# The opening of the full-attention layers: the first operands loaded ahead, the shift row written to SBUF, and the last keys and values cut into smaller pieces

## The chip, the cores and the metric

The kernel runs on one core of a Trainium2 chip. The metric is the device time of one execution in microseconds (us). The engines named below are PE (TensorE: matmuls), PEld (its weight loads), ACT (ScalarE), DVE (VectorE), POOL (GpSimd) and SP (SyncE), which here issues the DMAs.

## The reference

Four layers are chained: a windowed attention layer (A), a full one (B), then A and B again with the same weights. S = 2048 positions, D = 512, H = 32 heads of 16.

```python
def _B_ref(x, wqkv, wo):
    B, S, D = x.shape
    H = 32; Dh = D // H
    qkv = (lambda x, *d: x.transpose(*d))((x @ wqkv).reshape(B, S, 3, H, Dh), 2, 0, 3, 1, 4)
    q, k, v = qkv[0], qkv[1], qkv[2]
    scores = jnp.einsum("bhqd,bhkd->bhqk", q, k) * scale
    p = _softmax(scores, axis=-1)
    o = jnp.einsum("bhqk,bhkd->bhqd", p, v)
    return (lambda x, *d: x.transpose(*d))(o, 0, 2, 1, 3).reshape(B, S, D) @ wo
...
x = x + _A_ref(_layernorm(x, axis=-1), A_wqkv, A_wo)
x = x + _B_ref(_layernorm(x, axis=-1), B_wqkv, B_wo)
x = x + _A_ref(_layernorm(x, axis=-1), A_wqkv, A_wo)
x = x + _B_ref(_layernorm(x, axis=-1), B_wqkv, B_wo)
```

`_A_ref` is the same with a mask: a query sees itself and the 255 positions before it.

## The kernel before

**Tiling.** The positions are cut into 4 chunks of 512 (`c`), the heads into 4 head tiles of 8 (`ht`, `t`) or 8 quads of 4 (`qd`); two quads make a head tile. A projection of one chunk for one head tile is a pass of 12 matmuls (`mms`, L390: 4 slices of D times 3 products of split half-precision numbers). Q and K of a chunk are four such passes (`project`, L478); values (`values`, L607) go by four tiles of 128 positions, 12 matmuls each over all 32 heads (512 columns) or over a half of them (256 columns; `halves`, where 0 is the lower heads, used by quads 0 to 3, and 1 the upper).

**Keys, queries and the shift row.** Q and K are written to DRAM (`qs`, `kf`) in a layout of 64 rows a head (`R`), and loaded back by quad. Row 7 of a head in `kf` holds a shift, a bound from the largest squared norm of a key, that keeps the exponential in range. So the scores of a head cannot start before all keys of that head are known: `keys` (L553) leaves behind a piece of work in the list `pend`, which squares and sums the head's rows on PE (`squares`, L535) and reduces them on DVE to `KM` (L562); `settle` (L591) runs such pieces; `key_shift` (L595) takes the maximum over the chunks, makes the row `mk` (L602) and writes it to `kf` (L604). `queries` does the same for the query's own bound, a row `m` in `qs` (L588). `m` and `mk` share one buffer (tag "m").

**Full attention.** For a quad `load_full` (L744) loads `qt` (L748) and `kt` in two halves of 1024 keys (L752; three buffers). `attn_full` goes in 16 steps of 128 keys: two score groups on PE (L727), two exponentials on ACT (L735, 128x1024 each), and the products with V (L779). One layer has 4 x 8 x 16 = 512 steps and 1024 exponentials. Layer 1 goes by chunk of queries, then by quad; layer 3 by head tile, chunk, quad.

**Side work.** Work that isn't attention (projections, output projections, norms, for this layer or the next) is a list of `Work` generators. `Side` puts pieces of it between the attention steps: in a full layer `share` hands out a budget a step (`least`, 0.33 us of matmul by the code's own cost MM = 0.222 a pair), each pass writing into the one bank `halves`, which DVE reads out (`join`, L415 and L416). `finish` runs what is left without attention beside it, and `all_of` does that for a whole list. Weights of a work are loaded when it opens; there are two weight buffers, so a work opens when the one two before it is done. PE's order is the order in which this Python code issues; in the full layers DVE's too. The other engines, SP among them, are ordered by the planner.

**The way from a windowed layer to a full one.** After the last windowed attention the works of `tails[l]` and then `lasts[l]` run with no attention beside them: what depends on the output projection of chunk 3, its norm ("N") and its transposes ("T", DMA transposes at L470), and what else was put there. Then `key_shift` writes the row for all heads (layer 1) or for head tile 0 (layer 3, whose other tiles get theirs during the attention through `shift3`). Then the full attention begins with a load of `qt` and `kt`.

```python
tails = {0: [VV(1, 2, True, (0,)), OO(0, 3, True), VV(1, 1, True, (0,), late(1)), Q(1, 1, True, late(1)), T(1, 3), K(1, 3)],
         2: [VV(3, 0, True, (0,)), OO(2, 3, True), VV(3, 1, True, (0,), late(3)), VV(3, 2, True, (0,), late(3)), Q3(0, 0, True, late(3)), T(3, 3), K3(3, 0, True)]}
lasts = {0: [VV(1, 3)], 2: [VV(3, 3, True, (0,)), VV(3, 0, True, (1,))]}
```

`VV(l, c, act, halves, after, tiles)` are values, `OO(l, c)` the output projection of chunk c with the norm for the next layer, `Q` and `K` all four passes of a chunk, `Q3` and `K3` one pass (one head tile) with a slice of the weights.

Of the kernel before, what the change touches and what calls it, by code (L numbers as in the profile page):

```python
# [19 lines left out]
P = 128  # L20
# [4 lines left out]
QC = 512  # L25
# [164 lines left out]
def fast_path(ctx, tc, flag, a_x, a_wqkv, a_wo, b_wqkv, b_wo, out):  # L190
# [287 lines left out]
    def project(l, s, c, act, ht=None):  # L478
# [3 lines left out]
        w = weights(ty, s, n, *((0, D, 0) if ht is None else (ht * P, (ht + 1) * P, not act)))  # L482
# [112 lines left out]
    def key_shift(l, ht=None):  # L595

        settle()
        r = quarters(ht)
        kx = vp.tile([P, 1], F32, name=f"kx{l}_{ht}", tag="kx")
        nc.vector.tensor_reduce(kx[r], KM[l][r], axis=AX.X, op=ALU.max)  # L600
        m = vp.tile([P, QC], F16, name=f"mk{l}_{ht}", tag="m", bufs=1)
        nc.vector.tensor_scalar(m[r], ones[r], kx[r], -0.515, op0=ALU.mult, op1=ALU.mult)  # L602
        for t in range(NHT) if ht is None else (ht,):
            nc.sync.dma_start(rows(kf)[8 * t:8 * t + 8, 7, :].rearrange("h (c n) -> h c n", n=QC),  # L604
                              m[32 * t:32 * t + 8, None, :].broadcast_to([8, NQ, QC]))

    def values(l, c, act, halves=(0, 1), tiles=range(4)):  # L607
# [136 lines left out]
    def load_full(l, c, qd):  # L744
        n = f"{l}_{c}_{qd}"
        pair = slice(2 * qd, 2 * qd + 2)
        qt = pp.tile([P, 2, QC], F16, name=f"qt{n}", tag="qt", bufs=2)
        nc.sync.dma_start(qt, qs[1, c][pair].rearrange("r p n -> p r n"))  # L748
        kts = []
        for v in range(2):  # L750
# [69 lines left out]
    class Work:  # L820
# [34 lines left out]
        proj = property(lambda self: self.name is not None and self.name[0] in ("K", "Q", "K3", "Q3"))  # L855
# [130 lines left out]
    def attention(l, works):  # L986
# [5 lines left out]
        for t in range(NHT if l == 3 else 1):  # L992
            for c in range(NQ):
                qds = range(2 * t, 2 * t + 2) if l == 3 else range(NQD)
                if l == 1:

                    sd = sd or Side(NT * NQD // 2, works[0], works[1], 0.33)
                    while ("Q", 1, c) not in DONE:
                        sd.one(True)
# [4 lines left out]
                for qd in qds:  # L1004
                    if (l, c, qd) == (1, 0, NQD // 2):
                        sd.finish()
                        sd = Side(NT * NQD * NQ - NT * NQD // 2, works[1], works[2], 0.33)
                    nxt = load(l, c, qd + 1) if qd + 1 in qds else None
                    a = acc[qd % 2 if win else 0]
                    began, u = clock[0], 0  # L1010
                    for f in (attn_win if win else attn_full)(l, c, qd, *ops, a):
# [15 lines left out]
                        elif u:  # L1027
                            sd.step()
                        drain()
# [5 lines left out]
                if not win:  # L1035
                    settle()
# [14 lines left out]
    def K3(c, ht, act=False):  # L1051
        return Work(later(keys, 3, c, act, ht), PK / 4, ("K3", c, ht), [("T", 3, c)], True, ring=not act)
# [3 lines left out]

    def shift3(ht):
        def gen():
            key_shift(3, ht)
# [104 lines left out]

    def side1():
        m = [(ty, s) for ty in range(2) for s in range(4)]
        a = [CW(*x, [("C", *y)] if y else [("Q", 1, 2)]) for y, x in zip([None] + m, m)]
        a += [Q(1, c, False) for c in (2, 3)]
# [4 lines left out]
    def side3(t, c):  # L1173
        a = [Q3(c + 1, t)] if c < 3 else []
# [6 lines left out]
        if (t, c) != (0, 0):  # L1181
# [3 lines left out]
    works = [[side0(c) for c in range(NQ)], [[upper(1, c) for c in range(3)], side1()], [side2(c) for c in range(NQ)],  # L1185
             [side3(t, c) for t in range(NHT) for c in range(NQ)]]
    late = lambda l: [("N", l, 3)]
    tails = {0: [VV(1, 2, True, (0,)), OO(0, 3, True), VV(1, 1, True, (0,), late(1)), Q(1, 1, True, late(1)), T(1, 3), K(1, 3)],
             2: [VV(3, 0, True, (0,)), OO(2, 3, True), VV(3, 1, True, (0,), late(3)), VV(3, 2, True, (0,), late(3)), Q3(0, 0, True, late(3)), T(3, 3), K3(3, 0, True)]}
    lasts = {0: [VV(1, 3)], 2: [VV(3, 3, True, (0,)), VV(3, 0, True, (1,))]}  # L1190
    for l in range(4):
        if l % 2 == 0:
            attention(l, works[l] + [tails[l]])
            all_of(tails[l], lasts[l])
            key_shift(l + 1, 0 if l else None)
            all_of(lasts[l], works[l + 1][0])
        else:
# [43 lines left out]
```

## Time and profile before

| | us |
|---|---|
| three timed runs | 2759.93, 2760.06, 2761.41 (median 2760.06) |
| the profiled execution | 2759.5 |
| its span, first to last instruction | 2757.7 |
| PE busy | 2496.1 |
| ACT busy | 2362.9 |
| of it the exponentials (L735, 2432 of them) | 2238.8 |

The span starts at 0 in the profile's views. Rows of the timeline are: start, duration (both us), engine, line, operation, output and inputs, shapes, count of merged instructions, and in brackets the idle time ahead of it with what ended it. "SPq" rows are the issue of DMAs, not the transfers. Matmuls are pipelined: a matmul's duration is longer than the distance to the next.

### The profile page before, as it was taken

What the parts mean: (1) busy time and instruction counts of PE and PEld (TensorE: products, weight loads), DVE (VectorE), ACT (ScalarE), POOL (GpSimd) and SP (SyncE); (2) the same over time, 40 slices, a digit from 0 to 9 for tenths busy, and PEclk for the clock granted to TensorE, in tenths of its full rate; (3) what the DMA queues carried; (4) which work ended last, traced back from release to release, by engine and by line L of the source; (5) the groups of instructions that cost most, each with busy time, mean ns of one, the idle gap of its engine ahead of it and who ended that gap; (6) DMA issues with size and microseconds to landing.
All of it is one profiled execution on the core that took longest, in us unless ns stands there. A gap on an engine that the chain in (4) does not pass through costs nothing.

```text
span 2757.7 us, 112292 instructions
## 1 busy us (share of the span) xinstructions
PE 2496.1 (91%) x50513; PEld 1100.3 (40%) x50513; DVE 1094.9 (40%) x2314; ACT 2362.9 (86%) x2683; POOL 515.8 (19%) x1074
## 2 busy tenths in 40 slices
PE   7888989999989999999998898899899999998987
PEld 3233334444433344444443333534444444433332
DVE  5564554122343335325326566323333333333333
ACT  4556654899999999999995667399999999999997
POOL 1445552001000000100105678100000000000000
PEclk9999999999999999999999999999999999999999
DMA  8888856322342224324225565623232333333332
GB/s 286 226 241 240 244 178 191 96 83 82 100 120 79 86 93 137 102 78 126 93 73 169 157 181 143 175 72 109 84 107 90 98 97 104 112 104 123 114 120 103
DMA packets 335035, 359.67 MB, mean 130 GB/s; under 512 B 113616, under 2 KB 250320, under 8 KB 328144
## 3 DMA queue, kind: packets, MB, share of 16 engines
q1 hardware_dynamic: 334544, 352.40, 42.3%
q8 instruction: 397, 6.50, 1.0%
q14 instruction: 94, 0.77, 0.1%
HBM read 239.60 MB, written 96.99 MB: 122 GB/s over the span
## 4 chain that ended last, share of the span: by engine, by line
ACT 56%; PE 23%; issue 11%; DVE 5%; DMA 3%; POOL 2%; SPq 0%; ACTq 0%; DVEq 0%; POOLq 0%
ACT e L735 55%; PE b L402 10%; PE acc L812 3%; PE acc L779 3%; PE bs L402 2%; PE s L731 2%; PE s L727 2%; PE b L399 1%; POOL e L802 1%; POOL e L805 1%; DMA qt<-qs 1%; DMA kt<-kw 0%; DMA wr<-in_A_wo_dram 0%; DVE ot L694 0%; DMA w<-wd 0%
## 5 line engine op out<-in xcount | busy, mean ns | idle before, releaser
L735 ACT ACTIVATE e<-s 128x1024 f32<-128x1024 f32 (+2 forms) x2432 | 2238.8, 1058 | 121.0 <-PE s L731 95.3
L779 PE MATMUL acc<-e,vt 64*17 64x512 f32 x16384 | 1085.0, 590 | 1.3 <-issue 1.3
L727 PE MATMUL s<-qt,kt 64*32 64x512 f16 x16384 | 849.0, 380 | 130.4 <-ACT e L735 106.6
L727 PEld LDWEIGHTS <-kt 64*32 64x32 f16 x16384 | 406.7, 89 | 944.2 <-issue 868.8
L779 PEld LDWEIGHTS acc<-e,vt 64*17 64x17 f32 x16384 | 280.5, 92 | 61.1 <-issue 1.5
L805 POOL TENSOR_SCALAR_AFFINE_SELECT e<-e 128x256 f32<-128x256 f32 x512 | 224.9, 446 | 196.5 <-ACT e L735 195.4
L802 POOL TENSOR_SCALAR_AFFINE_SELECT e<-e 128x256 f32<-128x256 f32 x448 | 198.1, 449 | 114.1 <-ACT e L735 112.3
L712 POOL TENSOR_TENSOR oh<-o,oh 128x512 f16<-128x512 f32 x31 | 36.1, 1165 | 938.1 <-DVE oh L711 884.8
L812 PE MATMUL acc<-e,vt 128*17 128x384 f32 (+2 forms) x2816 | 204.7, 396 | 5.3 <-POOL e L802 4.0
L731 PE MATMUL s<-qt,kt 64*128 64x384 f16 (+2 forms) x1408 | 129.0, 280 | 64.0 <-ACT e L735 38.2
L415 DVE TENSOR_SCALAR sa<-acc 128x512 f32<-128x512 f32 x64 | 44.3, 692 | 335.4 <-PE acc L779 335.4
L402 PE MATMUL b<-xc,w 128*128 128x512 f16 x696 | 166.1, 390 | 7.0 <-DMA w<-wd 5.8
L677 DVE SCALAR_TENSOR_TENSOR x<-b,x 128x512 f32<-128x512 f32 x122 | 83.9, 688 | 193.0 <-PE b L399 189.8
L402 PEld LDWEIGHTS <-w 128*128 128x128 f16 x816 | 77.4, 100 | 122.8 <-issue 35.8
L521 POOL TENSOR_TENSOR sq<-sp 128x512 bf16<-128x512 f16 x28 | 41.0, 1463 | 442.2 <-DVE sp L515 427.6
L506 ACT ACTIVATE sp<-b 128x512 f16<-128x512 f32 x58 | 34.7, 598 | 103.3 <-PE b L402 91.2
L731 PEld LDWEIGHTS <-kt 64*128 64x128 f16 x1408 | 54.4, 94 | 167.6 <-issue 137.0
L521 POOL TENSOR_TENSOR sq_h<-sp_h 128x512 bf16<-128x512 f16 x27 | 40.1, 1484 | 409.8 <-DVE sp_h L515 409.8
L399 PE MATMUL b<-wo,oh 64*32 64x512 f16 x2592 | 109.9, 376 | 6.2 <-DVE x L677 3.1
L399 PE MATMUL b<-xc,w 64*32 64x512 f16 x2688 | 110.9, 376 | 3.0 <-DVE j L416 2.3
L399 PE MATMUL b<-xc,w_h 64*32 64x512 f16 x2592 | 104.4, 376 | 4.1 <-DVE km L562 3.9
L415 DVE TENSOR_SCALAR j_h<-b 128x512 f32<-128x512 f32 x27 | 18.7, 691 | 218.7 <-PE b L399 187.6
(136 smaller groups left out, 1874.8 us busy)
## 6 DMA issues: line engine op xcount, KB each, us to landing
kt<-kf SPq DMA_DIRECT2D x128, 512.0 KB
qt<-qs SPq DMA_DIRECT2D x128, 256.0 KB
xd<-x SPq DMA_DIRECT2D x96, 256.0 KB
x<-xd SPq DMA_DIRECT2D x96, 256.0 KB
w<-wd SPq DMA_DIRECT2D x22, 1024.0 KB
kt<-kw SPq DMA_DIRECT2D x64, 256.0 KB
qs<-sp SPq DMA_DIRECT2D x48, 256.0 KB
wo<-wd SPq DMA_DIRECT2D x12, 1024.0 KB
```

Of the source, the lines that this page charges most:

```text
L399: nc.tensor.matmul(ps[g:g + 32, r], a[k, g:g + 32], b[k], start=(i == 0), stop=(i == len(pairs) - 1), skip_group_check=True)
L402: nc.tensor.matmul(ps, a, b, start=(i == 0), stop=(i == len(pairs) - 1))
L415: nc.vector.tensor_scalar(dst, ps[0], scale, None, op0=ALU.mult)
L521: nc.gpsimd.tensor_tensor(sq, sp[:, 0], sp[:, 0], ALU.mult)
L677: nc.vector.scalar_tensor_tensor(xs[i], p, 1 / WS, xs[i], op0=ALU.mult, op1=ALU.add)
L727: nc.tensor.matmul(ps[g:g + 32, h], kt[R * h:R * h + R, pr, kc + g:kc + g + 32], qt[R * h:R * h + R, pr], start=True, stop=True, skip_grou ...
L731: nc.tensor.matmul(ps[:, h, s0:s0 + wd_], kt[R * h:R * h + R, pr, kc:kc + P], qt[R * h:R * h + R, pr, qc:qc + wd_], start=True, stop=True)
L735: nc.scalar.activation(e[:, :, w0:w1], ps[:, :, w0:w1], AF.Exp, scale=SCALE)
L779: nc.tensor.matmul(acc[r][32 * h:32 * h + DH + 1, :], V[l, qd // 4, j // 8][k, j % 8, 4 * (qd % 4) + h, :], es_[h // 2][k, h % 2, :], star ...
L802: nc.gpsimd.affine_select(v, v, pattern=[[0, 2], [-1, P]], compare_op=ALU.is_gt, fill=0.0, base=0, channel_multiplier=1)
L805: nc.gpsimd.affine_select(v, v, pattern=[[0, 2], [1, P]], compare_op=ALU.is_ge, fill=0.0, base=0, channel_multiplier=-1)
L812: nc.tensor.matmul(a[32 * h:32 * h + DH + 1, q * P:(q + nb) * P], V[l, (4 * c + j) // 4][:, j % 4, 4 * qd + h, :], es_[h // 2][:, h % 2, s ...
```

## The change

Four things, for both full layers:

1. `keys` gets an argument `then`, which is called with the head tile once its squares are reduced. A new work `K1(ht)` does the keys of layer 1's chunk 3 for one head tile and calls `key_shift` for it; `K3` does so for chunk 3 of head tile 0. `key_shift` works on one head tile at a time.
2. `early_keys` loads the first 1024 keys of the first quad into `kt` before the tail works, without a valid row 7. `early_queries` loads the first `qt`. For head tile 0 `key_shift` writes the row into that tile in SBUF (two DMAs, partitions 7 and 71) and then to `kf` as before; its row `mk` has a buffer of another tag. `load_full` takes what has been loaded.
3. The order of the tails. Layer 1: the values of chunk 1 with both halves and the upper values of chunk 0 come before the transposes of chunk 3; K of head tiles 0 and 1 follow, and two tiles of the lower values of chunk 3. Q of chunk 1, K of head tiles 2 and 3, two lower value tiles and the upper values of chunk 3 go to the attention's side work. Layer 3: the order of five works, and two lower value tiles of chunk 3 go to the side work.
4. Loops in `attention` run side work until what a quad needs is there: the shift of head tile 1, 2 or 3 before the load of quad 2, 4 or 6 of layer 1's first chunk, and the last two value tiles before step 11 of the first quad. `settle` isn't called while a pass is under way (`PH["busy"]`), and `values` calls it between tiles outside of attention.

```diff
-    def keys(l, c, act, ht=None):
+    def keys(l, c, act, ht=None, then=None):
...
                 nc.vector.tensor_reduce(KM[l][r, c:c + 1], ph[r], axis=AX.XY if PH["full"] else AX.X, op=ALU.max)
+                if then is not None:
+                    then(l, ht)
...
-    def key_shift(l, ht=None):
-
-        settle()
+    def key_shift(l, ht):
+
         r = quarters(ht)
         kx = vp.tile([P, 1], F32, name=f"kx{l}_{ht}", tag="kx")
         nc.vector.tensor_reduce(kx[r], KM[l][r], axis=AX.X, op=ALU.max)
-        m = vp.tile([P, QC], F16, name=f"mk{l}_{ht}", tag="m", bufs=1)
+        if PH["full"]:
+            m = vp.tile([P, QC], F16, name=f"mk{l}_{ht}", tag="m", bufs=1)
+        else:
+            m = vp.tile([P, QC], F32, name=f"mk{l}_{ht}", tag="j").bitcast(F16)[:, :QC]
         nc.vector.tensor_scalar(m[r], ones[r], kx[r], -0.515, op0=ALU.mult, op1=ALU.mult)
-        for t in range(NHT) if ht is None else (ht,):
-            nc.sync.dma_start(rows(kf)[8 * t:8 * t + 8, 7, :].rearrange("h (c n) -> h c n", n=QC),
-                              m[32 * t:32 * t + 8, None, :].broadcast_to([8, NQ, QC]))
+        if ht == 0:
+            early_queries(l)
+            for pr in range(2):
+                nc.sync.dma_start(PRE["k"][7:P:R, pr, :].rearrange("r (c n) -> r c n", n=QC),
+                                  m[2 * pr:2 * pr + 2, None, :].broadcast_to([2, 2, QC]))
+        nc.sync.dma_start(rows(kf)[8 * ht:8 * ht + 8, 7, :].rearrange("h (c n) -> h c n", n=QC),
+                          m[32 * ht:32 * ht + 8, None, :].broadcast_to([8, NQ, QC]))
+        DONE["S", l, ht] = clock[0]
+
+    PRE = {}
+
+    def early_keys(l):
+
+        PRE["k"] = pp.tile([P, 2, S // 2], F16, name=f"kt{l}_0_0_0", tag="kt", bufs=3)
+        nc.sync.dma_start(PRE["k"], kf[0:2, :, :S // 2].rearrange("r p n -> p r n"))
+
+    def early_queries(l):
+
+        if "q" not in PRE:
+            PRE["q"] = pp.tile([P, 2, QC], F16, name=f"qt{l}_0_0", tag="qt", bufs=2)
+            nc.sync.dma_start(PRE["q"], qs[1, 0][0:2].rearrange("r p n -> p r n"))
...
+            if not PH["full"] and not PH["win"]:
+                settle(False)
             yield -us if PH["full"] else -12 * us
...
-                    while ("Q", 1, c) not in DONE:
+                    while ("Q", 1, c) not in DONE or pend and PH["busy"]:
                         sd.one(True)
...
+                    while (l, c, qd % 2) == (1, 0, 1) and qd + 1 in qds and ("S", 1, (qd + 1) // 2) not in DONE:
+                        if ("K1", (qd + 1) // 2) in DONE and not PH["busy"]:
+                            settle()
+                        else:
+                            sd.one(True)
                     nxt = load(l, c, qd + 1) if qd + 1 in qds else None
...
+                        while not win and (c, qd, u) == (0, 0, NT - 5) and ("V", l, 3, (0,), 2) not in DONE:
+                            sd.one(True)
...
-                if not win:
+                if not win and not PH["busy"]:
                     settle()
...
+    def K1(ht, act=False):
+        return Work(later(keys, 1, NQ - 1, act, ht, key_shift), PK / 4, ("K1", ht), [("T", 1, NQ - 1), ("P", 1, 1)], True)
...
+    def last_lower(l):
+
+        return VV(l, 3, False, (0,), (), range(2, 4))
...
-        a += [Q(1, c, False) for c in (2, 3)]
+        a += [Q(1, c, False) for c in (1, 2, 3)]
...
     def side3(t, c):
-        a = [Q3(c + 1, t)] if c < 3 else []
+        a = [last_lower(3)] if (t, c) == (0, 0) else []
+        a += [Q3(c + 1, t)] if c < 3 else []
...
-    works = [[side0(c) for c in range(NQ)], [[upper(1, c) for c in range(3)], side1()], [side2(c) for c in range(NQ)],
+    works = [[side0(c) for c in range(NQ)], [[last_lower(1), K1(2), upper(1, 2), upper(1, 3), K1(3)], side1()], [side2(c) for c in range(NQ)],
...
-    tails = {0: [VV(1, 2, True, (0,)), OO(0, 3, True), VV(1, 1, True, (0,), late(1)), Q(1, 1, True, late(1)), T(1, 3), K(1, 3)],
-             2: [VV(3, 0, True, (0,)), OO(2, 3, True), VV(3, 1, True, (0,), late(3)), VV(3, 2, True, (0,), late(3)), Q3(0, 0, True, late(3)), T(3, 3), K3(3, 0, True)]}
-    lasts = {0: [VV(1, 3)], 2: [VV(3, 3, True, (0,)), VV(3, 0, True, (1,))]}
+    tails = {0: [VV(1, 2, True, (0,)), OO(0, 3, True), VV(1, 1, True, (0, 1), late(1)), VV(1, 0, True, (1,), late(1)), T(1, 3), K1(0, True), K1(1, True)],
+             2: [VV(3, 0, True, (0,)), OO(2, 3, True), Q3(0, 0, True, late(3)), VV(3, 1, True, (0,), late(3)), VV(3, 2, True, (0,), late(3)), VV(3, 0, True, (1,), late(3)), T(3, 3), K3(3, 0, True)]}
+    lasts = {l: [VV(l + 1, 3, True, (0,), (), range(2))] for l in (0, 2)}
...
             attention(l, works[l] + [tails[l]])
+            settle()
+            early_keys(l + 1)
+            if l == 0:
+                early_queries(1)
             all_of(tails[l], lasts[l])
-            key_shift(l + 1, 0 if l else None)
             all_of(lasts[l], works[l + 1][0])
+            settle()
```

More of the change, by code (lines that the diff above doesn't have):

```diff
@@ L481, in project @@
         ty, n = l % 2, f"{l}_{s}_{c}" + ("" if ht is None else f"_h{ht}")
-        w = weights(ty, s, n, *((0, D, 0) if ht is None else (ht * P, (ht + 1) * P, not act)))
+        w = weights(ty, s, n, *((0, D, 0) if ht is None else (ht * P, (ht + 1) * P, l == 3 and not act)))
         yield wait(8)
@@ L854, in fast_path @@
         done = begun = open = going = False
[L855 removed]
+        proj = property(lambda self: self.name is not None and self.name[0] in ("K", "Q", "K1", "K3", "Q3"))
         adds = property(lambda self: self.w and (self.name is None or self.name[0] == "N"))
@@ L1051, in K3 @@
     def K3(c, ht, act=False):
-        return Work(later(keys, 3, c, act, ht), PK / 4, ("K3", c, ht), [("T", 3, c)], True, ring=not act)
+        return Work(later(keys, 3, c, act, ht, key_shift if c == NQ - 1 and ht == 0 else None), PK / 4, ("K3", c, ht), [("T", 3, c)], True, ring=not act)
     def Q3(c, ht, act=False, after=()):
         return Work(later(queries, 3, c, act, ht), PK / 4, ("Q3", c, ht), [("T", 3, c), *after], True, ring=not act)
+    def K1(ht, act=False):
+        return Work(later(keys, 1, NQ - 1, act, ht, key_shift), PK / 4, ("K1", ht), [("T", 1, NQ - 1), ("P", 1, 1)], True)
     def shift3(ht):
         def gen():
+            settle()
             key_shift(3, ht)
```

12 lines of the change are left out of this document (7 added, 5 removed).

## The prediction

> **What bounds the kernel now.** First the page: its busy shares and the chain of waits.
>
> ```profile
> span 2757.7 us, 112292 instructions
> PE 2496.1 (91%) x50513; PEld 1100.3 (40%) x50513; DVE 1094.9 (40%) x2314; ACT 2362.9 (86%) x2683; POOL 515.8 (19%) x1074
> ACT e L735 55%; PE b L402 10%; PE acc L812 3%; PE acc L779 3%; PE bs L402 2%; PE s L731 2%; PE s L727 2%; PE b L399 1%; POOL e L802 1%; POOL e L805 1%; DMA qt<-qs 1%; DMA kt<-kw 0%; DMA wr<-in_A_wo_dram 0%; DVE ot L694 0%; DMA w<-wd 0%
> ```
>
> Over half of the chain is the exponential (L735). Next, the waits of ACT and of PE inside layer 1's attention (496 to 1448 us):
>
> ```profile
> ACT e L735 <- PE s L727: 7.1, 11, 1.7
> PE s L727 <- ACT e L735: 43.7, 119, 1.1
> PE b L399 <- DVE j L416: 3.0, 4, 0.8
> ```
>
> (Who waited for whom: us in total, times, longest.) In 952 us ACT waits for scores 11 times, 7.1 us in all: a full layer lasts as long as its 1024 exponentials. So the change can act at two places, where no exponential runs: from the last one of a windowed layer to the first of the full layer behind it. I read both in the timeline. Between layers 0 and 1:
>
> ```profile
> 432.00 4.82 ACT L735 ACTIVATE e<-s 128x1024 f32<-128x1024 f32 x5
> 439.04 1.48 PE L402 MATMUL bs<-wv,xc 128*128 128x256 f16 x12
> 454.65 1.47 PE L402 MATMUL bs<-wv,xc 128*128 128x256 f16 x12
> 460.12 2.76 PE L402 MATMUL bs<-xc,w 128*128 128x512 f16 x12
> 462.71 2.75 PE L402 MATMUL b<-xc,w 128*128 128x512 f16 x12
> 471.79 2.75 PE L402 MATMUL bs<-xc,w 128*128 128x512 f16 x12 [1.14 <-DMA xc<-xh]
> 484.09 0.38 PE L546 MATMUL b<-sq,hsum 128*32 128x512 bf16 x1 [1.02 <-ACT sq L519]
> 484.40 2.76 PE L402 MATMUL bs<-wv,xc 128*128 128x512 f16 x12
> 485.88 1.41 SPq L604 DMA_DIRECT2D kf<-mk_None  x4
> 489.60 1.41 SPq L752 DMA_DIRECT2D kt<-kf  x3
> 494.86 0.62 PE L727 MATMUL s<-qt,kt 64*32 64x512 f16 x16
> 495.51 24.86 ACT L735 ACTIVATE e<-s 128x1024 f32<-128x1024 f32 x27
> ```
>
> The last exponential ends at 436.82 and the next starts at 495.51: 58.7 us, in which PE is almost never idle (1.14 and 1.02 us). It is a queue of projections: values of chunk 2, output projection, values of chunk 1 (from 454.65), Q of chunk 1 (460.12), K of chunk 3 (471.79), values of chunk 3 (484.40). A pass of 12 matmuls over 512 columns takes 462.71 - 460.12 = 2.59 us; one over 256 columns half of it, 1.3 us. Between layers 2 and 3 the picture is another:
>
> ```profile
> 1725.09 1.94 ACT L735 ACTIVATE e<-s 128x1024 f32<-128x1024 f32 x2 [0.47 <-PE s L731]
> 1732.25 1.48 PE L402 MATMUL bs<-wv,xc 128*128 128x256 f16 x12
> 1748.05 0.53 SPq L370 DMA_DIRECT2D wv<-wd  x1
> 1757.25 0.69 DVE L448 TENSOR_TENSOR xh<-xn,xh 128x512 f16<-128x512 f32 x1
> 1765.56 4.45 PE L402 MATMUL bs<-xc,w_h 128*128 128x512 f16 x12 [3.79 <-DMA x<-xd]
> 1771.35 0.38 PE L546 MATMUL bs<-sq_h,hsum 128*32 128x512 bf16 x1 [1.03 <-ACT sq_h L519]
> 1774.48 0.34 DVE L602 TENSOR_SCALAR mk<-ones,kx 32x512 f16<-32x512 f16 x1 [1.86 <-DMA qs<-m]
> 1777.53 1.41 SPq L752 DMA_DIRECT2D kt<-kf  x3
> 1783.07 0.63 PE L727 MATMUL s<-qt,kt 64*32 64x512 f16 x16 [0.75 <-DMA kt<-kf]
> 1783.61 4.69 ACT L735 ACTIVATE e<-s 128x1024 f32<-128x1024 f32 x5 [0.87 <-PE s L727]
> ```
>
> Here 56.6 us pass from 1727.03 to 1783.61. K of the last chunk starts 3.79 us late and in 4.45 us instead of 2.59, the shift row waits 1.86 us for its tile, and the first scores wait for the load of `kt` behind the shift row. That load and two weight loads, in the chain of waits:
>
> ```profile
> 454.84 5.22 DMA w<-wd
> 1755.22 3.42 DMA w_h<-wd
> 1777.53 5.49 DMA kt<-kf
> ```
>
> 1 MB of weights takes 5.22 us and a 256 KB slice 3.42; a half-width `wv` (512 KB) I put between, at 4.
>
> **Layer 1's start, step by step.** Values of chunk 2 and the output projection stay: PE is at 454.65. Values of chunk 1 with both halves are 4 x 2.59 = 10.4, upper values of chunk 0 4 x 1.3 = 5.2: 470.3. In this time the norm and the transposes of chunk 3, which landed at 471.7 before, are done; two 1 MB weight loads no longer run beside them, so I take them as hidden under the 5.2 (if not, +1.4). K of head tiles 0 and 1, 2.59 each. The ring has two buffers: tile 0's slice is asked for at 465.1 (in time); tile 1's at 470.3, so at 473.7 + 0.1, 0.9 after tile 0 ends at 472.9; it ends at 476.4. Tile 0's squares stand behind it on PE (0.4). From squares to shift row the old rows show 485.88 - 484.09 = 1.8, so the two small writes into SBUF are issued at 478.2 and 478.6. Their landing is not in the trace; the nearest row is the old shift's: last issue about 487.3, reload 489.60, so 2.3; the far one is the 5.49 of a 512 KB load. They carry 4 KB each, so I take 2.3: 480.9. Meanwhile PE does the two value tiles of chunk 3: weights asked for at 472.9, there at 476.9, 2 x 1.3 and the second squares 0.4 from then on: 479.9. So scores at 481.0 and the first exponential 0.65 later, 481.6: **-13.9**, of which PE's shorter queue is 13. Bounds: PE alone without waits 439.04 + 39.8 = 478.8 and 479.6 with the exponential (-15.9); the far landing and the late transposes 485.7 (-9.8).
>
> The early `kt` and `qt` loads are put on SP right after the windowed attention. What is queued behind them there is the weights of chunk 1's values, needed at 454.65, ten us after their buffer comes free: cost 0; a load that waits for its slot would eat this cover first. The other `kt` half now follows the shift row: 480.9 + 5.5 = 486.4, and is read 8 steps after 481, at 496 (24.86 us for 27 exponentials, two a step: 1.84). Hidden.
>
> **Layer 3's start.** PE from 1732.25: values 5.2, output projection 10.4, Q of tile 0 2.6: 1750.5. The next `wv` is asked for at 1748.05 as now, and lands at 1752.1: 1.6 lost. Three half-width values, 15.7, end at 1767.8; the third's weights come in the same stretch as the transposes, so 0.8 more: 1768.6. K is then covered (the last `xh` is ready at 1757.94, and its weights are asked for at 1762.6), no idle time stands ahead of it, and it takes 2.59: 1771.2. The last values' weights are asked for at 1768.6, land at 1772.6; one tile 1.3, then the squares at 1773.9, shift row issued 1775.7, behind the `qt` load (0.4) 1776.1 and 1776.5, landed 1778.8, first exponential 1779.3: **-4.3**. Q's `m` is no longer in the shift row's way (the 1.86). Bounds: without any of these weight waits 1775.4 (-8.2); with a landing of 5.49 and 0.4 of queue 1782.5 (-1.1).
>
> **What moves into the attention.** Layer 1 gains Q of chunk 1 (10.4), K of tiles 2 and 3 (5.2), two lower value tiles of chunk 3 (2.6) and its upper values (5.2), and loses the upper values of chunks 0 and 1 (10.4): 13.0 us of PE, what the tail saved. Layer 3 gains 2.6. What hides it is seen in two steps of layer 1:
>
> ```profile
> 505.00 0.41 PE L727 MATMUL s<-qt,kt 64*32 64x512 f16 x8
> 505.76 0.41 PE L727 MATMUL s<-qt,kt 64*32 64x512 f16 x8 [0.35 <-ACT e L735]
> ...
> 507.05 0.63 PE L399 MATMUL b<-wv,xc 64*32 64x256 f16 x32
> 507.59 0.41 PE L727 MATMUL s<-qt,kt 64*32 64x512 f16 x8
> ```
>
> Between the two scores of a step are 0.76 us; without side work PE waits in it, with 32 side matmuls (about 0.4) the next scores still start on time. The code hands out 0.33 a step, 169 us in 512 steps; the layer's side work was 157 by the code's own costs and becomes 171, so 0.34 a step: cost 0. What goes is a slack of 11 us in the second quarter of the steps; the third and fourth held 43 us in 128 steps already. The deadlines: value tiles by step 8 at this pace (needed at 11), K of tile 2 by 16 (at 48), K of tile 3 by 57 (at 80), Q by about 98 (at 128). With the work move its loads and writes on SP and, for the K tiles, two small DVE operations and a write each for their shift rows. The stretch in which Q of chunks 2 and 3 run now shows what the transfers meet there:
>
> ```profile
> 634.00:680.00 46.00, 43.85 (x1104) 1.00 0.23 74
> 467.00:470.00 3.00, 3.00 (x15) 1.00 1.16 232
> ```
>
> (Columns: stretch, its length, PE busy, granted clock, DMA share, GB/s; the second row is the transposes ahead of layer 1.) The DMA share is 0.23: hidden. PE shows 43.85 of 46, but eight of these matmuls run side by side, so the steps above tell more than this share.
>
> One term remains: PE is less busy as each full layer opens.
>
> ```profile
> 1784.00:1787.00 3.00, 1.31 (x32) 0.94 0.69 208
> 1787.00:1790.00 3.00, 3.00 (x47) 0.50 0.03 5
> ```
>
> ```profile
> 1789.31 1.02 ACT L735 ACTIVATE e<-s 128x1024 f32<-128x1024 f32 x1 [1.01 <-PE s L727]
> ```
>
> Layer 3 opened with PE busy 1.31 of 3 us, then ran 3 us at clock 0.50, and ACT waited 1.01 us for scores. Layer 1 opens in the same way now: **+1.2** (0 to 2.4).
>
> A page rule against it: the Trainium skill, TensorE: Matmul & The Clock Gate, section What's actually happening, says that the clock falls to half after a whole idle window of about 3.4 us. PE's wait in layer 1 is 1.1 us, so by the rule this term is 0 and the time 1.2 less; the trace shows the drop after a stretch that was not idle throughout, and the sum goes by the trace.
>
> **Sum**, against the profiled execution's 2759.5: -13.9 - 4.3 + 1.2 = -17.0, so 2742.5; the median of the runs shown, 2760.06, lies 0.6 above it. I say 2742.5.
>
> **Rivals.** (1) The two starts are set by small transfers, not by PE: transposes as late as now, the shift row landing like a full load. -9.8 - 1.1 + 1.2: 2749.8. For it: DMA is the last releaser ahead of the first scores of layer 3, and the transfer engines are full (1.16) while the transposes run; against: two 1 MB loads leave that stretch, and the rows are tiny.
> (2) Slower: the new loops do run. They issue side work with no scores between, so ACT stands still for each pass and for its bank: a pass costs 2.59 + 0.75 (PE's waits at L399 for DVE, 3.0 in 4). Six passes of Q and K, 6 x 3.3 = 20.0, and four value tiles at 2.05 in both layers, 8.2: +28.2 - 18.2 + 0 = 2769.5. It turns the sign once about two thirds of this work is forced. For it: all of it has a deadline at a quad, and K must be followed by squares; PE at 43.85 of 46 too; against: the pace above, and 7.1 us of ACT waits in the whole layer.
> (3) Only the deadlines of the first quads fail: the weights of the last value tiles are asked for when K is done, a few steps before they are needed, and K of tiles 2 and 3 queue up behind them. 8.2 + 2 x 3.3 = 14.8 comes back: 2756.1, no difference that can be told. For and against it stands the same, with the least room, 3 steps, at the value tiles.
>
> **Numbers.** Forecast 0.58, (1) 0.22, (2) 0.11, (3) 0.09. Faster by over 0.2% (some 5.5 us; what a measurement of this kernel can tell from no change): forecast and (1), 0.80; within: (3), 0.09; slower: (2), 0.11. Range: the low end is both PE-only starts, -15.9 - 8.2 = 2735.4; the high end is (1) with 2.4 for the clock and some 4 us of forced passes, 2755.
>
> **What would show it.** Right: 44 to 46 us without exponentials at the first place and 52 at the second; the first scores of each full layer wait for the small write; no wait for K's transposed input; each full layer takes as long as now from its first exponential to its last. Wrong: ACT gaps of over 2 us ahead of quads 1, 2, 4 or 6 of layer 1, or in its last quarter; first scores that wait for a weight load or for SP.

## The result and the profile after

| | before | after |
|---|---|---|
| median of seven runs, us | 2760.06 (2757.61 to 2764.27) | 2751.53 (2743.84 to 2753.62) |
| ratio | | 0.9966 (0.9955 to 0.9977), 8.5 us less |
| profiled execution, us | 2759.5 | 2743.84, the lowest of its seven |

The kernel is faster by 0.3%, about half of what was forecast. The page of the kernel after (span and chain of waits):

```profile
span 2742.0 us, 113349 instructions
ACT e L759 55%; PE b L402 10%; PE acc L837 3%; PE acc L804 3%; PE s L755 2%; PE s L751 2%; PE bs L402 2%; PE b L399 1%; POOL e L827 1%; POOL e L830 1%; DMA wv<-wd 0%; DVE xh L448 0%; DMA kt<-kw 0%; DVE ot L718 0%; DVE xn L442 0%
```

In its code the exponential is L759, the first score groups L751, the maximum over chunks L601, the row `mk` L606, its write into `kt` L610, that to `kf` L612, the load of `kt` L777, of `qt` L774. The load of `kt` behind the shift row is no longer in the chain; a weight load (`wv`) has come in. The two places without exponentials, first the one ahead of layer 1, in the timeline:

```profile
429.89 4.82 ACT L759 ACTIVATE e<-s 128x1024 f32<-128x1024 f32 x5
436.92 1.48 PE L402 MATMUL bs<-wv,xc 128*128 128x256 f16 x12
452.53 2.75 PE L402 MATMUL bs<-wv,xc 128*128 128x512 f16 x12
462.89 1.47 PE L402 MATMUL bs<-wv,xc 128*128 128x256 f16 x12
464.42 1.24 SPq L470 DMA_TRANSPOSE xc<-xh  x1
466.44 2.40 SPq L370 DMA_DIRECT2D w_h<-wd  x2
470.00 2.76 PE L402 MATMUL bs<-xc,w_h 128*128 128x512 f16 x12 [1.71 <-DMA w_h<-wd]
472.80 0.52 SPq L370 DMA_DIRECT2D wv<-wd  x1
475.29 0.39 PE L546 MATMUL bs<-sq_h,hsum 128*32 128x512 bf16 x1
477.89 1.48 PE L402 MATMUL b<-wv,xc 128*128 128x256 f16 x12 [2.21 <-DMA wv<-wd]
479.73 0.68 DVE L562 TENSOR_REDUCE km<-bs 32x1 f32<-32x512 f32 x1 [2.67 <-PE bs L546]
480.44 0.34 DVE L606 TENSOR_SCALAR mk<-ones,kx 32x512 f16<-32x512 f16 x1
480.81 1.27 SPq L610 DMA_DIRECT2D kt<-mk  x2
482.62 0.41 PE L751 MATMUL s<-qt,kt 64*32 64x512 f16 x8 [1.52 <-DMA kt<-mk]
483.16 3.77 ACT L759 ACTIVATE e<-s 128x1024 f32<-128x1024 f32 x4 [1.64 <-PE s L751]
```

From 434.71 to 483.16 are 48.5 us, where 58.7 stood. The first scores wait for the small write, as forecast; but PE has two new waits for weights ahead of them, 1.71 and 2.21 us. The `km` row at 479.73 is the second head tile's reduction, and the first tile's `mk` stands behind it on DVE: the row leaves 5.5 us after its squares (475.29 to 480.81), where 1.8 was taken. Ahead of layer 3:

```profile
1711.31 1.94 ACT L759 ACTIVATE e<-s 128x1024 f32<-128x1024 f32 x2 [0.47 <-PE s L755]
1718.64 1.49 PE L402 MATMUL b<-wv,xc 128*128 128x256 f16 x12
1734.45 0.53 SPq L370 DMA_DIRECT2D wv<-wd  x1
1739.14 1.21 PEld L402 LDWEIGHTS <-xc 128*128 128x128 f16 x12 [2.63 <-DMA wv<-wd]
1741.15 2.74 PE L402 MATMUL bs<-wv,xc 128*128 128x256 f16 x12
1745.94 3.31 SPq L470 DMA_TRANSPOSE xc<-xh  x2
1749.30 0.59 SPq L370 DMA_DIRECT2D wv<-wd  x1
1753.59 1.49 PE L402 MATMUL b<-wv,xc 128*128 128x256 f16 x12 [1.78 <-DMA wv<-wd]
1758.84 2.75 PE L402 MATMUL b<-xc,w_h 128*128 128x512 f16 x12
1763.14 1.48 PE L402 MATMUL bs<-wv,xc 128*128 128x256 f16 x12 [1.55 <-DMA wv<-wd]
1764.56 0.39 PE L546 MATMUL b<-sq_h,hsum 128*32 128x512 bf16 x1
1766.24 1.21 SPq L610 DMA_DIRECT2D kt<-mk  x2
1767.97 0.41 PE L751 MATMUL s<-qt,kt 64*32 64x512 f16 x8 [1.61 <-DMA kt<-mk]
```

1713.25 to 1768.51 are 55.3 us, where 56.6 stood. K (1758.84) no longer waits for its input, as forecast, but each of three sets of value weights is late. (The first wait is read from the weight loads, PEld. The matmul's own row, at 1739.15, names the DVE row of `nb`, which ended last; in slices_apart the same tile starts 2 us before `nb` is made, so it doesn't need it.) What the span is made of, from the first and last exponential of each layer (192 in layers 0 and 2, 1024 in 1 and 3); "again" kernels are unchanged copies that ran with the experiments:

| us | layer 0 | ahead of 1 | layer 1 | ahead of 2 | layer 2 | ahead of 3 | layer 3 |
|---|---|---|---|---|---|---|---|
| before | 382.8 | 58.7 | 951.5 | 1.5 | 278.5 | 56.6 | 954.2 |
| before_again | 383.7 | 58.4 | 952.3 | 1.5 | 278.6 | 56.2 | 954.1 |
| after | 379.8 | 48.5 | 950.7 | 3.0 | 276.3 | 55.3 | 953.6 |
| again | 383.8 | 48.4 | 950.4 | 3.0 | 276.3 | 55.1 | 953.7 |
| again2 | 387.3 | 48.0 | 951.1 | 3.0 | 276.5 | 57.3 | 954.5 |

(The start takes 54 to 55 us more, the end 20.) The opening of layer 1 gives 10.3 us by the means of these executions, that of layer 3 only 0.5, and the full layers are no longer than before. Layer 0, which the change doesn't touch, differs by 7.5 us between executions of one kernel. The first profile of after has the shortest one, 3.0 us below before's, so its own 2743.84 lies closer to the forecast's 2742.5 than the kernel does.

### The profile page after: what moved, and what is told of

Same layout as the page of the kernel before. It is cut to its first block, busy times and chain, and to the rows that moved or that the text cites. A ratio compares the mean times of both kernels' runs of the same rounds, so it can differ in the third digit from the quotient of the medians.

```text
span 2742.0 us, 113349 instructions
## 1 busy us (share of the span) xinstructions
PE 2493.2 (91%) x51023; PEld 1103.0 (40%) x51023; DVE 1110.8 (41%) x2342; ACT 2356.7 (86%) x2671; POOL 521.8 (19%) x1080
## 3 DMA queue, kind: packets, MB, share of 16 engines
q1 hardware_dynamic: 340664, 353.46, 43.3%
## 4 chain that ended last, share of the span: by engine, by line
ACT 56%; PE 23%; issue 11%; DVE 5%; DMA 2%; POOL 2%; SPq 0%; ACTq 0%; DVEq 0%; POOLq 0%
ACT e L759 55%; PE b L402 10%; PE acc L837 3%; PE acc L804 3%; PE s L755 2%; PE s L751 2%; PE bs L402 2%; PE b L399 1%; POOL e L827 1%; POOL e L830 1%; DMA wv<-wd 0%; DVE xh L448 0%; DMA kt<-kw 0%; DVE ot L718 0%; DVE xn L442 0%
## 5 line engine op out<-in xcount | busy, mean ns | idle before, releaser
L759 ACT ACTIVATE e<-s 128x1024 f32<-128x1024 f32 (+2 forms) x2432 | 2239.5, 1057 | 121.4 <-PE s L755 99.1
L751 PE MATMUL s<-qt,kt 64*32 64x512 f16 x16384 | 851.0, 380 | 121.7 <-ACT e L759 99.1
L751 PEld LDWEIGHTS <-kt 64*32 64x32 f16 x16384 | 406.7, 89 | 929.2 <-issue 848.4
L755 PE MATMUL s<-qt,kt 64*128 64x384 f16 (+2 forms) x1408 | 129.0, 280 | 59.5 <-ACT e L759 38.2
L402 PE MATMUL b<-xc,w 128*128 128x512 f16 x660 | 156.9, 389 | 6.6 <-DMA w<-wd 5.4
L399 PE MATMUL b<-xc,w 64*32 64x512 f16 x3072 | 127.7, 376 | 3.0 <-DVE j L416 1.5
L399 PE MATMUL b<-xc,w_h 64*32 64x512 f16 x2784 | 111.2, 376 | 4.7 <-DVE km L562 3.9
L402 PEld LDWEIGHTS <-w 128*128 128x128 f16 x720 | 68.2, 100 | 109.3 <-issue 33.1
L415 DVE TENSOR_SCALAR vt<-b 128x256 f32<-128x256 f32 (+1 forms) x36 | 18.4, 512 | 228.7 <-PE b L399 228.7
```

The source lines that it names most:

```text
L399: nc.tensor.matmul(ps[g:g + 32, r], a[k, g:g + 32], b[k], start=(i == 0), stop=(i == len(pairs) - 1), skip_group_check=True)
L402: nc.tensor.matmul(ps, a, b, start=(i == 0), stop=(i == len(pairs) - 1))
L415: nc.vector.tensor_scalar(dst, ps[0], scale, None, op0=ALU.mult)
L751: nc.tensor.matmul(ps[g:g + 32, h], kt[R * h:R * h + R, pr, kc + g:kc + g + 32], qt[R * h:R * h + R, pr], start=True, stop=True, skip_grou ...
L755: nc.tensor.matmul(ps[:, h, s0:s0 + wd_], kt[R * h:R * h + R, pr, kc:kc + P], qt[R * h:R * h + R, pr, qc:qc + wd_], start=True, stop=True)
L759: nc.scalar.activation(e[:, :, w0:w1], ps[:, :, w0:w1], AF.Exp, scale=SCALE)
```

## The experiments

My theory after the result: layer 1's opening gives the whole gain, layer 3's next to none; both fell short because PE waits for weights, which have only two buffers and are issued in SP's order; the moved work is hidden. Rivals: the gain is given back inside the full layers, or the early load of `kt` does nothing.

**The same kernels again.** `again` and `again2` are the changed kernel unaltered, `before_again` the old one.

> The changed kernel once more. Its profiled execution took 2743.8 us and the other six 2750.2 to 2753.6. Theory A (the change acts at the two openings alone; the 7.7 us are half-clock stretches of PE in the windowed layers, which it does not touch): the median is again about 2751, the stretch without exponentials ahead of layer 1 is 48.5 us and ahead of layer 3 55.3 us in this trace too, the full layers take 950 to 951 and 953 to 954 us from first to last exponential, and what differs from the first trace lies in layers 0 and 2. Rival B (the work moved into the attention costs several us in most executions): an execution of about 2751 us shows layer 1 or 3 longer by 5 us or more.

> The kernel before once more, for the spread of its parts. Theory A: the stretches ahead of layers 1 and 3 are 58.7 and 56.6 us and the full layers 951 and 954 us, each within 0.5 us of the first trace; layers 0 and 2 differ by up to some us. Rival B says the same of this kernel.

> The changed kernel a third time, one execution, for its parts: the first two traces took 2743.8 and 2746.7 us, the unprofiled executions mostly 2749 to 2753. If the executions differ in half-clock stretches of PE, this one shows the two openings at 48.4 and 55.2 us within 1 us, the full layers within 3 us, and what is above 2744 in layers 0 and 2 and in the first steps of the full layers.

Measured: again 2749.38 (2746.72 to 2752.78, nine runs), ratio 0.9972 (0.9962 to 0.9982), which is 7.7 us gained, or 8.8 by the two medians; before_again 2760.70; again2 2754.88. The profiled executions average 2748.5 for three of after and 2760.1 for two of before, 11.6 apart; the timed medians say 8 to 9. Differences of a few us between single executions are no evidence; the two openings repeat within 0.5 (ahead of layer 1) and 2.2 us, and ahead of layer 3 again2 misses what was expected of it (57.3 for 55.2). The expectation put the rest down to half clock in the windowed layers. For layer 0 this holds in part at most: the granted clock over it is 0.95 in after and 0.93 in again, which is 4.0 us longer, but also 0.93 in again2, which is 3.5 us longer still.

**One full layer alone.** The order of the tails, the early load, the writes into `kt` and the new side work for one layer, the old code for the other:

```diff
-    PRE = {}
+    PRE, NEW = {}, (1,)
...
-        if ht == 0:
+        if ht == 0 and l in NEW:
             early_queries(l)
...
+            if l + 1 not in NEW:
+                settle()
+                key_shift(l + 1, 0 if l else None)
             all_of(lasts[l], works[l + 1][0])
```

> The change for layer 1 alone; the tail and the opening of layer 3 as before. Theory A (openings add up: 10.2 us at layer 1, 1.3 at layer 3): about 2752 us in median, 1 above the whole change; ahead of layer 1 48.5 us, ahead of layer 3 56.6. Rival B (moved work costs in the attention): the gain here is under 8 us and layer 1 is longer than 953 us.

> The change for layer 3 alone; the tail and the opening of layer 1 as before. Theory A: about 2759 us in median, 1 below the kernel before; ahead of layer 3 55.3 us, with four waits of PE for weights (2.1, 1.8, 1.6 us) and the shift row (1.6 us) in it. By the prediction's sum it would be 2756.

Measured: layer1_only 2750.32, ratio 0.9974 (0.9965 to 0.9984), with 47.4 us ahead of layer 1, 57.6 ahead of layer 3 and 953.1 in layer 1; layer3_only 2758.76, ratio 1.0005 (0.9996 to 1.0014), with 56.2 us ahead of layer 3, where 55.3 was expected. By the letter layer1_only shows the sign of rival B: a gain under 8 us (7.8 by the medians) and a layer 1 over 953. But layer 1 took 949.2 us in layer3_only and 951.5 and 952.3 in before, all without the moved work, so 2 us of one execution tell nothing; and its two longest ACT waits behind the opening, 2.6 us in step 139 and 1.0 in step 316, stand at no deadline of the moved work. Layer 1's half carries all that can be told of the gain; layer 3's forecast -4.3 is outside this interval (-1.1 to +3.9 us).

**Without the early loads.** The order of the works as after, the first `kt` and `qt` loaded behind the shift row as in before:

```diff
-        if ht == 0:
+        if ht == 0 and "k" in PRE:
...
             settle()
-            early_keys(l + 1)
-            if l == 0:
-                early_queries(1)
             all_of(tails[l], lasts[l])
```

> The change without its early loads: the shift row goes to the keys in DRAM alone and the first quad's operands are loaded behind it, as before; the shorter tails and the moved side work stay. If the shift row's way sets the start (it did by the trace: the first scores waited 1.5 and 1.6 us for the small write), the load now follows it, 5.5 us and the write's landing, in place of a landing of 1.8: the stretches ahead of layers 1 and 3 are about 54.5 and 61 us in place of 48.4 and 55.2, and the median about 2762, above the kernel before. Rival: PE's queue sets the start and the early load is worth little: both stretches stay within 2 us, about 2752.

Measured: 2763.45, ratio 1.0015 (1.0001 to 1.0029); 54.1 us ahead of layer 1, 60.9 ahead of layer 3. The timeline of no_early:

```profile
492.08 1.05 PE L751 MATMUL s<-qt,kt 64*32 64x512 f16 x16 [6.29 <-DMA kt<-kf]
```

PE waits 6.29 us for the load. The early load is worth 5.7 and some 5 us at the two places; without it the rest of the change shortens the first place by 4.5 us and lengthens the second by as much (58.6 and 56.4 before, on average), and the kernel gains nothing.

**Q of chunk 1 back in the tail.** `Q(1, 1)` stands behind the upper values of chunk 0 again and leaves the side work:

```diff
-        a = [CW(*x, [("C", *y)] if y else [("Q", 1, 1)]) for y, x in zip([None] + m, m)]
-        a += [Q(1, c, False) for c in (1, 2, 3)]
+        a = [CW(*x, [("C", *y)] if y else [("Q", 1, 2)]) for y, x in zip([None] + m, m)]
+        a += [Q(1, c, False) for c in (2, 3)]
...
-    tails = {0: [VV(1, 2, True, (0,)), OO(0, 3, True), VV(1, 1, True, (0, 1), late(1)), VV(1, 0, True, (1,), late(1)), T(1, 3), K1(0, True), K1(1, True)],
+    tails = {0: [VV(1, 2, True, (0,)), OO(0, 3, True), VV(1, 1, True, (0, 1), late(1)), VV(1, 0, True, (1,), late(1)), Q(1, 1, True, late(1)), T(1, 3), K1(0, True), K1(1, True)],
```

> The change with Q of layer 1's chunk 1 put back into the tail, behind the upper values. If the moved work is hidden in the attention, layer 1 keeps its 950 to 951 us from first to last exponential, and the stretch ahead of it grows from 48.4 by four passes (10.4) and a square (0.4), less up to 2 us of weight waits that they cover: 57 to 59 us. Rival: the move cost something in the attention; then layer 1 gets shorter by some us here.

Measured: 2760.44 (one run), 59.5 us ahead of layer 1, layer 1 953.5 us. The opening grows by 11 us, its four passes and a little, and layer 1 does not get shorter for being rid of them: inside the layer this Q costs nothing, as the prediction had it. The 3.0 us ahead of layer 2 are 1.5 again here, so that shift goes with this Q in the side work. The shorter layer 2 (276.3 to 276.5 after, 278.5 before) doesn't: it is 277.0 here, and 278.7 in slices_apart below, where the Q is in the side work. Its length goes with the time that the trace grants it half clock: 6.8 us in the five traces with 278.4 to 279.1 us (both of before, layer3_only, no_early, slices_apart), 3.4 us in the seven with 276.3 to 277.2, none in layer1_only with 275.1.

**The first shift row ahead of the second tile's squares.** In layer 1 the pending squares are no longer run between the two last value tiles:

```diff
-            if not PH["full"] and not PH["win"]:
+            if not PH["full"] and not PH["win"] and l == 3:
                 settle(False)
```

> The second head tile's squares are put behind the last value tile of layer 1's tail, so that on DVE the first shift row is no longer queued behind their reduction. If that queue made the row 3.4 us late, the row is written 1.8 us after the first squares, PE's own queue sets the start, and the stretch ahead of layer 1 is 47.0 us in place of 48.4; the first scores wait for no write. Rival: the row waits for something else; the stretch stays at 48.4 and the row comes 5 us after its squares.

Measured: 2746.58 (one run), 47.8 us ahead of layer 1. The timeline and two stretches (length, PE busy, granted clock, DMA share, GB/s) of mk_first:

```profile
480.31 1.27 SPq L610 DMA_DIRECT2D kt<-mk  x2
480.60 2.34 PE L402 MATMUL b<-wv,xc 128*128 128x256 f16 x12 [2.14 <-DMA wv<-wd]
485.31 0.63 PE L751 MATMUL s<-qt,kt 64*32 64x512 f16 x16
```

```profile
477.00:480.50 3.50, 1.46 (x7) 1.00 0.97 271
480.50:484.00 3.50, 3.40 (x18) 0.58 0.75 221
```

The row leaves SP at 480.31, and the scores at 485.31 wait for nothing. But the place shows no gain that can be told: 47.8 us, where after took 48.0 to 48.5 and q_later (below), whose layer 1 is that of after, 47.9; 47.0 was expected. The value tiles wait 2.14 for their weights and then run at little more than half clock. The weights come first, the row's order second.

**Layer 3's Q later.** If the first wait for weights is only a matter of which work stands where, Q behind the values of chunk 2 should take it away:

```diff
-             2: [VV(3, 0, True, (0,)), OO(2, 3, True), Q3(0, 0, True, late(3)), VV(3, 1, True, (0,), late(3)), VV(3, 2, True, (0,), late(3)), VV(3, 0, True, (1,), late(3)), T(3, 3), K3(3, 0, True)]}
+             2: [VV(3, 0, True, (0,)), OO(2, 3, True), VV(3, 1, True, (0,), late(3)), VV(3, 2, True, (0,), late(3)), Q3(0, 0, True, late(3)), VV(3, 0, True, (1,), late(3)), T(3, 3), K3(3, 0, True)]}
```

> Layer 3's tail in another order: Q of head tile 0 behind two values in place of ahead of them, so that the weights of the values are asked for one work earlier. If the waits for weights are what the prediction missed at layer 3, the wait of 2.1 us behind the output projection and the half-clock stretch after it go, and the stretch ahead of layer 3 is about 52 us in place of 55.2. Rival: the waits move to the other works and it stays within 1 us.

This theory fell: 2750.04 (one run), and 57.4 us ahead of layer 3. The timeline of q_later:

```profile
1751.50 0.54 SPq L370 DMA_DIRECT2D wv<-wd  x1
1756.52 1.87 PE L402 MATMUL bs<-wv,xc 128*128 128x256 f16 x12 [4.42 <-DMA wv<-wd]
```

The wait is longer, 4.42 us: the buffer was free when the values of chunk 2 were through, at 1747.7, but on SP the load stood behind the transposes and loads of `x`, 3.8 us more. Another order of the works only moves the wait to another load.

**The slices in buffers of their own.** The four 256 KB slices of the openings (K of tiles 0 and 1 of layer 1, Q and K of tile 0 of layer 3) use the slice buffers that stand idle there, so that they can be loaded long before and the value weights keep both of their own buffers. `Q3` and `K3` get `ring` in the same way as `K1`; mk_first's edit is in it too:

```diff
+    EARLY = {(1, 1, 3, 0), (1, 1, 3, 1), (3, 0, 0, 0), (3, 1, 3, 0)}
...
-        w = weights(ty, s, n, *((0, D, 0) if ht is None else (ht * P, (ht + 1) * P, l == 3 and not act)))
+        w = weights(ty, s, n, *((0, D, 0) if ht is None else (ht * P, (ht + 1) * P, (l, s, c, ht) in EARLY or l == 3 and not act)))
...
-                    (len(wused[self.ring]) < RINGS[self.ring] or wused[self.ring][-RINGS[self.ring]].done) and (PH["full"] or not self.ring)
+                    (len(wused[self.ring]) < RINGS[self.ring] or wused[self.ring][-RINGS[self.ring]].done) and (not PH["win"] or not self.ring)
...
-        return Work(later(keys, 1, NQ - 1, act, ht, key_shift), PK / 4, ("K1", ht), [("T", 1, NQ - 1), ("P", 1, 1)], True)
+        return Work(later(keys, 1, NQ - 1, act, ht, key_shift), PK / 4, ("K1", ht), [("T", 1, NQ - 1), ("P", 1, 1)], True, ring=(1, 1, NQ - 1, ht) in EARLY)
```

> The four weight slices of the tails (Q and K of one head tile) get the buffers of the other ring, which stand free there, so that no work of the tails waits for weights; and the second squares stand last as in mk_first. If weights and the row's queue on DVE are all that PE waited for, the stretches ahead of layers 1 and 3 are about 43 and 47.6 us in place of 48.4 and 55.2, some 13 us less in all: about 2738 in median. Rival: the transposes of chunk 3 or the small write take the place of the weights, and less than half of it is won.

Measured: 2744.17 (2741.95 to 2748.01), ratio 0.995 (0.9937 to 0.9964); 43.3 us ahead of layer 1, 50.9 ahead of layer 3. That is 14.9 us below before by the medians and so some 6 below after, less than half of the 13 expected, which was the rival's sign. The two openings give 9 to 10 of the 13; the full layers of this trace (952.1 and 955.4) are 1 to 2 us longer than those of after, and why stays open. The timeline of slices_apart, where L752 is the first scores:

```profile
440.05 1.48 PE L402 MATMUL bs<-wv,xc 128*128 128x256 f16 x12
471.26 2.75 PE L402 MATMUL bs<-xc,w_h 128*128 128x512 f16 x12
480.58 0.41 PE L752 MATMUL s<-qt,kt 64*32 64x512 f16 x8 [0.61 <-DMA kt<-mk]
...
1751.29 2.75 PE L402 MATMUL b<-xc,w_h 128*128 128x512 f16 x12 [1.72 <-DMA xc<-xh]
1761.83 0.39 PE L546 MATMUL bs<-sq_h,hsum 128*32 128x512 bf16 x1
1763.52 1.19 SPq L610 DMA_DIRECT2D kt<-mk  x2
1765.28 0.41 PE L752 MATMUL s<-qt,kt 64*32 64x512 f16 x8 [3.05 <-DMA kt<-mk]
```

Ahead of layer 1 no wait for weights is left, and the theory's figure is met. Ahead of layer 3 the weight waits are gone too, but K now runs early (1751.29) and its squares only 8 us behind it, after six value tiles: the work list goes on with K, which hands its squares over at its end, only when the values listed ahead of it are through. PE then stands 3.05 us for the row, behind 1.72 us for the transposes: ahead of layer 3 the rival had it right.

**K ahead of the last values.** slices_apart with K of layer 3 one place further forward:

```diff
-             2: [VV(3, 0, True, (0,)), OO(2, 3, True), Q3(0, 0, True, late(3)), VV(3, 1, True, (0,), late(3)), VV(3, 2, True, (0,), late(3)), VV(3, 0, True, (1,), late(3)), T(3, 3), K3(3, 0, True)]}
+             2: [VV(3, 0, True, (0,)), OO(2, 3, True), Q3(0, 0, True, late(3)), VV(3, 1, True, (0,), late(3)), VV(3, 2, True, (0,), late(3)), T(3, 3), K3(3, 0, True), VV(3, 0, True, (1,), late(3))]}
```

> slices_apart with K of layer 3's last chunk listed ahead of the upper values of chunk 0, so that its generator is resumed, and its squares are handed on, while those values still run; in slices_apart the squares came only behind all six value tiles and PE then stood 3.05 us for the shift row. If that hand-over is what was left, the row is written behind the third value tile, lands before PE is done, and the stretch ahead of layer 3 is about 47.7 us in place of 50.9; the median about 2741. Rival: the transposes (1.72 us in slices_apart) or the row's landing hold it; it stays at 50 or more.

Measured: 2738.29 (2737.69 to 2740.93), ratio 0.993 (0.9916 to 0.9944), 20.9 us below before and 11 to 13 below the medians of after; 43.3 us ahead of layer 1, 48.0 ahead of layer 3. The timeline of k_ahead, where L760 is the exponential:

```profile
1750.02 2.75 PE L402 MATMUL b<-xc,w_h 128*128 128x512 f16 x12 [1.73 <-DMA xc<-xh]
1756.72 0.39 PE L546 MATMUL b<-sq_h,hsum 128*32 128x512 bf16 x1
1758.40 1.19 SPq L610 DMA_DIRECT2D kt<-mk  x2
1761.07 0.95 PE L752 MATMUL s<-qt,kt 64*32 64x512 f16 x16
1761.61 4.69 ACT L760 ACTIVATE e<-s 128x1024 f32<-128x1024 f32 x5
```

The first scores wait for nothing; what is left is 1.73 us for the transposes. This version beats both kernels.

## Why the prediction came out as it did

The direction, the places and the mechanism were right; the time lies in the range, 9 us above the forecast, and the gain is half of the one forecast. Of its own signs three came: the first scores wait for the small write, K doesn't wait for its input, and the full layers keep their length. The two lengths did not: 48.5 and 55.3 us, where 44 to 46 and 52 were named. Offsets below are from PE's first projection of the place (439.04 in before, 436.92 in after; 1732.25 and 1718.64).

- **PE's shorter queue in layer 1, 13 us: right.** Putting Q alone back costs 11 (q_in_tail), and with the weight waits gone the place is 15.4 us shorter than in before's profile (slices_apart), close to the bound of 15.9. Its K starts at 31.2 us, the forecast said 31.3.
- **The step that failed there: "tile 0's slice is asked for at 465.1 (in time)".** That is 26.1 us in; it was issued at 29.5. Its buffer was free when the values of chunk 1 were through, at 462.89, but SP issued a transpose at 464.42 and a load of `x` at 465.70 first, so K started 1.8 us late. The value weights wait for K's buffer in turn: there at 41.0 instead of 37.9, 2.0 of it from the late issue (472.80, 35.9 in, for 33.9) and 1.1 from a load of 5.1 us (472.80 to 477.88) where 4 was taken. The shift row, 1.8 us from squares to issue, had to stand behind the second tile's squares and reduction on DVE: 0.6 more in this trace (mk_first, without that queue, gained too little to confirm it). 2.0 + 1.1 + 0.6 = 3.7, the whole gap between -13.9 and -10.2. I had costed the moved steps on PE and read the buffers, but not written out SP's order behind the transposes nor DVE's.
- **Layer 3, -4.3: the steps right, the waits mis-sized.** The values behind the output projection start 20.5 us in, not 19.9 (+0.7); the half clock after that wait takes 1.3 (in again2 and layer3_only the same wait, 2.1 us, has full clock behind it) and the squares of Q with their wait, which the sum left out, 0.7; the third values' weights cost 1.95 instead of 0.8 (+1.15), since their buffer was free at 1745.1, when the values of chunk 1 were through, but SP issued transposes until 1749.25 and the load only then; the last ones +0.45. The row made good 1.5, since the `qt` load was no longer in its way and it landed in 1.73 us. Sum 2.8, and 0.2 at its start: 52.3 became 55.3. In again2 the wait for the third values' weights was 3.8 us and the place 57.3, so what this opening gains lies between 1.3 us and a loss of about 1.

```profile
1761.92 2.26 PE L402 MATMUL b<-wv,xc 128*128 128x256 f16 x12 [3.82 <-DMA wv<-wd]
```

(The row is of again2's timeline.) That the weights are the cause is shown by slices_apart. Ahead of layer 1 it differs from mk_first (47.8) by the buffers of the slices alone and reaches 43.3, under the forecast's 44.8. Ahead of layer 3 it takes away the waits for weights and with them 4 us or more (50.9, under the forecast's 52.3); the last 2.9 us, to 48.0, are K's place in k_ahead.
- **Early loads at no cost, the small landing: right.** No wait arose from the early loads at the values of chunk 1, and no_early shows their worth. The landing measured 1.81 (480.81 to 482.62) and 1.73 us, below the 2.3 taken; rival (1)'s price, a landing like a full load, fell, although its 2749.8 is nearer to the time that came than the forecast: it had the size, not the cause.
- **Moved work at no cost: right**, and rivals (2) and (3) fell. Layer 1 takes 950.4 to 951.1 us in after's three traces (951.5 and 952.3 before); in the experiments it spreads from 949.2 to 953.5 with and without the moved work, so a cost under some 2 us could not be seen. ACT's waits from its first to its last exponential (us in total, times, longest), in after:

```profile
ACT e L759 <- PE s L751: 5.2, 9, 1.6
```

5.2 us from 484.5 on, against 7.1 before, and the one of 1.6 us is at 743, behind the first chunk of queries (128 steps from 483 on, at 1.86 us a step) and with it behind every deadline of the moved work: no quad is held up for it.
- **The half clock at layer 1's opening, +1.2: it exists, smaller.** The stretches (length, PE busy, granted clock, DMA share, GB/s) of after, first ahead of and in layer 1's opening, then around layer 3's first weight wait:

```profile
481.00:484.50 3.50, 1.19 (x25) 0.98 0.18 36
484.50:487.50 3.00, 3.00 (x80) 0.50 0.90 250
...
1737.00:1740.50 3.50, 1.36 (x13) 0.99 0.94 292
1740.50:1743.90 3.40, 3.40 (x17) 0.50 0.70 233
```

ACT lost 0.58 us for it at 488 (0.68 in again, 1.10 in again2), and the layer as a whole is not longer, so this term was too large by a tenth to a half. Layer 3 no longer has the like: its wait of 1.01 us at 1789 in before has no counterpart in after, which the sum left out. The drop came at a place where the sum had none, the weight wait of layer 3 (1.3 us). By the rule weighed in the prediction (the Trainium skill, TensorE: Matmul & The Clock Gate, section What's actually happening) neither drop should be there, since no idle time ahead of them fills its window of about 3.4 us: the longest are 1.52 and about 2.3. The trace disagrees with it.

## What to carry to other kernels

When work is taken out of a stretch where one engine is the bound, write out the order of the next resources as well: which buffer each weight load waits for, what stands ahead of it on its queue, and which reduction stands ahead of the small result everyone waits for. An early operand pays in full only if nothing else is late at the same point. Here the change brought 8 to 9 us, and giving the small slices idle buffers of their own, with K placed so that its squares follow at once, brought 12 us more. Where executions of one kernel differ by ten us, compare stretches of the trace that the change touches, not the ends.

## What the runs showed of the hardware

- Half clock needs no long idle wait. After stretches of 3.4 or 3.5 us in which PE was busy for 1.19, 1.36 (after) or 1.46 us (mk_first), the next 3 to 3.5 us were granted 0.50 to 0.58, and no single idle time in them was over 2.3 us. It doesn't follow every such wait: again2 and layer3_only kept full clock behind the 2.1 us. In k_ahead the opening of layer 3 does it (the same columns):

```profile
1761.40:1764.80 3.40, 1.59 (x40) 0.95 0.89 260
1764.80:1768.20 3.40, 3.40 (x72) 0.55 0.84 281
```

- A small write into SBUF, two DMAs issued in 1.2 to 1.3 us, was usable 1.73 to 1.83 us after its first issue, at each place and in each kernel where PE waited for it.
- Layer 0, with the same work everywhere, took 379.8 to 387.3 us in executions of the same kernel; the granted clock (0.95 and 0.93) goes with a part of it at most, and where the rest goes stays open.
